# Closing the MLP's small tiles early and reordering the first four token tiles in a fused attention and MLP kernel

## Chip, cores and metric

The kernel runs on one core of a Trainium2 chip. The metric is the device time of one execution in microseconds (us). The engines are named as the profile names them: PE is TensorE (PEld its weight loads), DVE is VectorE, ACT is ScalarE, POOL is GpSimd, SP is SyncE, which here only issues transfers.

## What is computed

A layer norm of x feeds two branches, whose outputs are added to x: a recurrent attention over 64 segments of 32 tokens that carries 8 memory rows from segment to segment, and a dense MLP with GELU.

```python
x = A_x                      # 1 x 2048 x 1024, bf16
xn = _layernorm(x, axis=-1)
return x + _A_ref(xn, A_mem0, A_Wq, A_Wk, A_Wv, A_Wo, 32) + _B_ref(xn, B_w1, B_b1, B_w2, B_b2)

# _A_ref, for each of the 64 segments:
h = concat([mem, xs])                     # 8 + 32 rows
q, k, v = h @ Wq, h @ Wk, h @ Wv          # 32 heads of 128
p = softmax(where(mask, q @ k.T * scale, -1e9))
o = (p @ v) @ Wo
mem = o[:, :8]                            # goes to the next segment
# _B_ref: gelu(xn @ w1 + b1) @ w2 + b2, with 3584 hidden columns
```

## The kernel before

**Two stages.** The MLP is done first (lines 299 to 614), then a loop over the 64 segments (line 691 on). The four attention matrices are cut into 64 units of 512 KB each. 46 of them stay in SBUF for the whole loop (resident). 18 are streamed: two are copied from PSUM by DVE, and 16 are transferred again from DRAM in each segment, one of these only in part. Streamed units live in six slots (`RING`); when PE has used one, `start_stream` (line 246) issues the transfer of the unit that is due six places later into the same slot.

**The first token tiles.** The MLP goes over four groups of four token tiles (128 tokens each). For a tile, `ln_stats` (line 348) makes two `bn_stats` of 512 columns and an aggregate on DVE, `ln_sqrt` a square root on ACT and `ln_rstd` a reciprocal on DVE. The normalised tile `ln_xn` is then made by `ln_apply_scalar` on ACT (line 371) for tiles 0 to 2 of the first group, and by `ln_apply` on DVE (line 363) for tile 3. `turn_x` (line 383) turns it with eight PE transposes into PSUM and copies it out in two halves, one on ACT and one on DVE. `begin`, `normed` and the loop at line 472 order these so that the statistics of tile t+1 come ahead of the application of tile t. Only after all four tiles does PE begin the first product (line 509): for each of 28 blocks of hidden columns (`fb`), eight matmuls of 512 columns. ACT, DVE and ACT again then make the GELU.

**SP's queue** holds its transfers in program order and waits at the first one that may not go yet. Apart from these waits the program lets each hardware transfer wait for the one issued eight before it. At the start the order is: four tiles of x, two pairs of w1, the bias `b1rows`, the other pairs of w1, then w2.

**Where the units go.** SBUF is full during the MLP. When the last group (`tg == 3`) has used a piece of w1, w2 or the GELU result `gT`, its place is given to a resident unit: `fetch_resident("w1_..")` at line 535 and, within the last second products (line 595: 28 steps `fc`, eight matmuls each), `w2_..` at line 606 and `gT..` at line 608. Four units (`LATE`, tiles `W_O..`, parts of Wo) have no such place. They go into the pool `late` (line 621), which takes the address range that the MLP's small tiles (pool `ma`: `g_xb`, `g_u`, `ln_xn`, `ones`, `b2row` and others) had, and so is opened after `ma` is closed. Their transfers, then those of two units in `xt2` and `xt3`, are put in `late_units` (line 672), and `unit_done` (line 675) issues one of them after each streamed unit that the first segment uses:

```python
            if IS_STREAMED[unit]:
                start_stream(slot_of.pop(place_in_stream.pop(unit)))
                if late_units:
                    late_units.popleft()()
```

`xt2` and `xt3` hold the last four token tiles until `keep_R` has stored them (`R_n`, issued by ACT at line 415), so their transfers wait for these stores.

**The first segment** (s = 0) makes nearly every product twice (for the rows of the segment, `hr_home`, and for rows left over from the neighbours, `hrL`). The order of the passes is K, Q, K, Q, V, V and then the output product O.

**The end.** In the last segment the result leaves in 12 small transfers, dealt out in turn to SP, ACT and POOL (line 1049).

Of the kernel before, what the change touches and what calls it, by code (L numbers as in the profile page):

```python
# [51 lines left out]
LATER = 3  # L52
LAG = 3
STREAM_BUFS = 6
AT_BANKS, AT_PART = 5, 4
PART_COLS = 768

# [30 lines left out]
def kernel(  # L88
# [208 lines left out]


    NT = S // P
    with tc.tile_pool(name="ma", bufs=2) as ma, tc.tile_pool(name="mps", bufs=6, space=PSUM) as mps:  # L300
        eps_t = ma.tile([P, 1], F32, name="eps_t", bufs=1)
        nc.vector.memset(eps_t[:], EPS)
        ones = ma.tile([1, P], BF16, name="ones", bufs=1)
# [21 lines left out]
                w1_sb.append(t)  # L325

        b1rows = ma.tile([FC, P], BF16, name="b1rows", bufs=1)
        load_w1(range(2))
        nc.sync.dma_start(out=b1rows[:, :], in_=B_b1.rearrange("(fc p) -> fc p", p=P))
        load_w1(range(2, 6))  # L330
        masks_out()
        for j in range(4):
            nc.sync.dma_start(
# [11 lines left out]
        mv = ma.tile([P, NT, 2], F32, name="ln_mv", bufs=1)  # L345
        rstd = ma.tile([P, NT], F32, name="ln_rstd", bufs=1)

        def ln_stats(tt, xt):
            stats = ma.tile([P, 2, 6], F32, name="ln_stats")
            for c in range(2):  # L350
                nc.vector.bn_stats(out=stats[:, c, :], in_=xt[:, c * 512:c * 512 + 512])
            nc.vector.bn_aggr(out=mv[:, tt, :], in_=stats[:, :, :])

        def ln_sqrt(t0, t1):
            nc.scalar.activation(
                out=rstd[:, t0:t1], in_=mv[:, t0:t1, 1:2].rearrange("p t o -> p (t o)"), func=ACT.Sqrt,
                bias=eps_t[:, :], scale=1.0,
            )
# [9 lines left out]
            )  # L368
            return xn

        def ln_apply_scalar(tt):

            xn = ma.tile([P, DM], BF16, name="ln_xn")
            shift = mv[:, tt, 0:1]
            nc.vector.tensor_scalar(
                out=shift, in0=shift, scalar1=rstd[:, tt:tt + 1], scalar2=-1.0, op0=ALU.mult, op1=ALU.mult,
            )
            nc.scalar.activation(
                out=xn[:, :], in_=xtoks[tt], func=ACT.Identity, bias=shift, scale=rstd[:, tt:tt + 1],
            )  # L380
            return xn

        def turn_x(tt, xn, xnT):
            t = tt % 4
            pT = mps.tile([P, KT, P], BF16, name="pT", bufs=2)
            for kt in range(KT):
                nc.tensor.transpose(pT[:, kt, :], xn[:, kt * P:(kt + 1) * P], ident)
            for half in range(2):
                cp = nc.scalar.copy if (tt + half) % 2 else nc.vector.tensor_copy
                cp(  # L390
                    out=xnT[half][:, 4 * t:4 * t + 4, :, :].rearrange("p s k t -> p k s t"),
                    in_=pT[:, 4 * half:4 * half + 4, :].rearrange("p k (s t) -> p k s t", t=SEG),
                )

        def keep_xT(tg, xnT):
            xl = [sp.tile([P, 2, KT, GRP, NL], BF16, name="xl", tag=("a", "kL0")[k]) for k in range(2)]
# [62 lines left out]
            ]  # L459

        xnT = new_xnT(0)
        def begin(tt):
            ln_stats(tt, xtoks[tt])
            ln_sqrt(tt, tt + 1)

        def normed(tt):
            ln_rstd(tt, tt + 1)
            return ln_apply_scalar(tt) if tt < 3 else ln_apply(tt)

        begin(0)  # L470
        xns = []
        for tt in range(4):
            if tt < 3:
                begin(tt + 1)
            xns.append(normed(tt))
            if tt > 0:
                turn_x(tt - 1, xns[tt - 1], xnT)
        turn_x(3, xns[3], xnT)
        keep_xT(0, xnT)

        b1col = ma.tile([P, FC], F32, name="b1col", bufs=1)
# [6 lines left out]
        for tg in range(4):  # L488
# [16 lines left out]

            pend = None
            for fb in range(FC):
                ps = mps.tile([P, 512], F32, name="ps")
                for kt in range(KT):
                    nc.tensor.matmul(  # L510
                        ps[:, :].rearrange("p (s t) -> p s t", t=SEG),
                        lhsT=w1_sb[fb // 2][:, kt, (fb % 2) * P:(fb % 2 + 1) * P],
                        rhs=xnT[kt // 4][:, :, kt % 4, :],
                        start=(kt == 0),
                        stop=(kt == KT - 1),
                    )
                xb = ma.tile([P, 512], BF16, name="g_xb", bufs=3)
                nc.scalar.activation(  # L518
                    out=xb[:, :], in_=ps[:, :], func=ACT.Identity, bias=b1col[:, fb:fb + 1], scale=1.0
                )  # L520
                u = ma.tile([P, 512], BF16, name="g_u")
                nc.vector.tensor_tensor(out=u[:, :], in0=xb[:, :], in1=xb[:, :], op=ALU.mult)
                nc.vector.tensor_scalar(
                    out=u[:, :], in0=u[:, :], scalar1=0.044715, scalar2=1.0, op0=ALU.mult, op1=ALU.add
                )
                nc.vector.tensor_tensor(out=u[:, :], in0=u[:, :], in1=xb[:, :], op=ALU.mult)  # L526
                if pend is not None:
                    gelu_tail(*pend)
                pend = (fb, u, xb)
                if last and fb % 2:  # L530
                    place = f"w1_{fb // 2}"
                    if place in RING:
                        start_stream(place)
                    else:
                        fetch_resident(place)
# [9 lines left out]
            if not last:  # L545
# [5 lines left out]
                        fetch(c, unit)  # L551
                    fetch_resident(*EARLY)
                for t in range(4):
                    ln_stats(4 * tg + 4 + t, xtoks[4 * tg + 4 + t])
                ln_sqrt(4 * tg + 4, 4 * tg + 8)
                ln_rstd(4 * tg + 4, 4 * tg + 8)
                for t in range(4):
# [22 lines left out]
            else:  # L580
# [8 lines left out]
                for n in range(8):  # L589
                    cs = slice((n % 2) * 512, (n % 2 + 1) * 512)  # L590
                    nc.tensor.matmul(pss[n][:, :], lhsT=ones[0:1, :], rhs=b2row[0:1, cs], start=True, stop=False)
                    nc.tensor.matmul(
                        pss[n][:, :], lhsT=ident, rhs=xtoks[4 * tg + n // 2][:, cs], start=False, stop=False
                    )
                for fc in range(FC):
                    for t in range(4):
                        for nb in range(2):
                            nc.tensor.matmul(
                                pss[2 * t + nb][:, :],
                                lhsT=gts[fc // 4][:, fc % 4, t * P:(t + 1) * P],  # L600
                                rhs=w2_sb[fc // 2][:, fc % 2, nb * 512:nb * 512 + 512],
                                start=False,
                                stop=(fc == FC - 1),
                            )
                    if fc % 2:
                        fetch_resident(f"w2_{fc // 2}")
                    if fc % 4 == 3:
                        fetch_resident(f"gT{fc // 4}")
# [9 lines left out]

    with tc.tile_pool(name="late", bufs=1) as late, \
            tc.tile_pool(name="banks", bufs=1, space=PSUM) as banks:
        nc.scalar.preload_act_table_set("natural_log_exp_and_others")

        small = deque()
# [38 lines left out]
                return stream_tiles.pop(used - 1)[:, :]  # L664
            return res_tiles[unit]

        def fetch_late(unit):
            t = late.tile([P, 2048], BF16, name="W_" + "_".join(map(str, unit)))[:, :]
            res_tiles[unit] = t
            fetch(t, unit)  # L670

        late_units = deque(lambda unit=unit: fetch_late(unit) for unit in LATE)
        late_units += [lambda: fetch_resident("xt2"), lambda: fetch_resident("xt3")]

        def unit_done(unit):

# [14 lines left out]
        for s in range(NSEG):  # L691
# [354 lines left out]
            ]  # L1046
            left_rows = [(sl, row) for sl, row in left_rows if row >= 0]
            if final:
                engines = [nc.sync, nc.scalar, nc.gpsimd]
                n = 0  # L1050
                for w, r in enumerate(tiles):
                    for b in range(2):
                        cs = slice(256 * (2 * b + w), 256 * (2 * b + w) + 256)
                        pieces = [(rows, slice(64 * b + m0, 64 * b + m0 + NX))]
                        for sl, row in left_rows:
                            p0 = 64 * b + NL * sl
                            pieces.append((slice(row, row + NL), slice(p0, p0 + NL)))
                        for o, i in pieces:
                            engines[n % 3].dma_start(out=out_flat[o, cs], in_=r[i, :])
                            n += 1  # L1060
            elif left_o:
                pairs = [(out_flat[rows, :], outL_d[og, m0:m0 + NX, :])]
                pairs += [
                    (out_flat[row:row + NL, :], outL_d[og, NL * sl:NL * sl + NL, :]) for sl, row in left_rows
                ]
                for o, r in pairs:
                    small.append(lambda o=o, r=r: nc.gpsimd.dma_start(out=o, in_=r))
            else:
                for j in range(4):
                    nc.gpsimd.dma_start(out=out_flat[rows, 256 * j:256 * j + 256], in_=res[32 * j:32 * j + NX, :])  # L1070
# [37 lines left out]
```

## Time and profile before

| | us |
|---|---|
| three runs | 1865.07, 1869.99, 1869.29 (median 1869.29) |
| profiled execution | 1868.06 |
| its span, first to last instruction | 1866.3 |
| begin of the first product of the MLP | 15.99 |
| end of the last second products | 418.2 |
| first product of the segment loop | 419.35 |
| last matmul | 1859.84 |
| PE busy, share of the span | 92% |
| DVE, ACT, POOL busy | 48%, 35%, 15% |
| bytes moved by transfers | 613 MB |

The profile gives busy times of the engines, and a chain of waits that is followed back from the last instruction. A matmul's row has a start and a modelled end, and the ends of neighbours overlap: the distance of starts is the rate at which they go. In a timeline, "x8" is a merged row of eight instructions, and the bracket names the idle time before it and what ended it. DMA share is the mean busy share of 16 transfer engines; it can be a little over 1. Times are counted from the start of the span.

### The profile page before, as it was taken

The page shows a single profiled execution, that of the slowest core. Times are in us where ns is not written, and L with a number is a line of the kernel's source. Part 1 is how long each engine was busy: PE and PEld are TensorE (multiplying, and loading weights), DVE is VectorE, ACT ScalarE, POOL GpSimd, SP SyncE. Part 2 cuts the span into 40 slices and gives each one's busy share as a digit, 9 for nine tenths or more (in the row PEclk, how much of TensorE's full clock was granted, in tenths as well). Part 3 has the DMA queues.
Part 4 walks back from the last instruction along what each step waited for, and adds up shares of the span by engine and source line. Part 5 has one row for each costly group of instructions (what it writes and reads, how often), then busy time and mean ns, then how long its engine had stood idle before and what let it go on. Part 6 is the DMA issues. An engine that isn't in the chain of part 4 may idle for free.

```text
span 1866.3 us, 72877 instructions
## 1 busy us (share of the span) xinstructions
PE 1720.2 (92%) x32208; PEld 938.3 (50%) x32228; DVE 905.1 (48%) x2192; ACT 649.4 (35%) x1382; POOL 286.7 (15%) x563
## 2 busy tenths in 40 slices
PE   7999999999999999998899999999898898999987
PEld 3444444445555555555554555555555454545544
DVE  6657483705444444444444444444444444445443
ACT  6434251602333333333333333333333333333333
POOL 0000001401341121111111111111111111111112
PEclk9999999999999999999999999999999999999999
DMA  9921212769999999999999999999999999999998
GB/s 290 311 83 47 54 46 60 255 217 388 401 394 380 395 390 384 387 380 371 369 383 368 390 388 390 365 384 374 379 389 360 369 368 377 387 389 394 388 381 315
DMA packets 229353, 613.13 MB, mean 329 GB/s; under 512 B 46859, under 2 KB 76091, under 8 KB 229036
## 3 DMA queue, kind: packets, MB, share of 16 engines
q1 hardware_dynamic: 207260, 588.06, 83.8%
q0 software_dynamic: 17536, 17.71, 2.9%
q8 instruction: 252, 4.13, 0.9%
q10 hardware_dynamic: 4240, 2.71, 0.5%
q14 instruction: 65, 0.53, 0.1%
HBM read 594.40 MB, written 29.23 MB: 334 GB/s over the span
## 4 chain that ended last, share of the span: by engine, by line
PE 40%; DMA 20%; issue 4%; DVE 4%; ACT 2%; POOL 0%; DVEq 0%; ACTq 0%; SPq 0%; POOLq 0%
PE acc L715 27%; PE acc L919 9%; DMA u<-Wc_K 8%; DMA u<-Wc_O 7%; DMA outL_d<-half_home 2%; PE acc L891 1%; DMA u<-Wc_Q 1%; ACT mixed L865 1%; DVE b_oL L780 1%; PE mixed L824 1%; DVE pd_main L872 1%; DMA u<-Wc_V 1%; DMA hr_home<-hr_d 1%; ACT mixed L862 0%; PE mixed L830 0%
## 5 line engine op out<-in xcount | busy, mean ns | idle before, releaser
L715 PE MATMUL acc<-u,hr_home 128*32 128x512 bf16 x11520 | 781.3, 381 | 36.6 <-issue 13.8
L715 PEld LDWEIGHTS <-hr_home 128*32 128x32 bf16 x12288 | 353.3, 96 | 321.8 <-issue 69.7
L715 PE MATMUL acc<-u,hrL 128*32 128x512 bf16 x2880 | 258.7, 383 | 7.7 <-issue 7.3
L510 PE MATMUL ps<-u 128*128 128x512 bf16 x896 | 195.5, 381 | 2.6 <-ACT u L390 2.6
L244 DVE TENSOR_SCALAR u<-kept 128x512 uint32<-128x512 uint32 x254 | 163.4, 685 | 33.1 <-PE acc L715 11.1
L919 PE MATMUL acc<-u,d_oL 128*32 128x256 bf16 (+1 forms) x3108 | 157.6, 290 | 22.5 <-DMA u<-Wc_O 12.8
L565 PE MATMUL ps<-u 128*128 128x512 bf16 x657 | 146.2, 379 | 0.8
L919 PEld LDWEIGHTS <-b_oL 128*32 128x32 bf16 x3569 | 112.8, 98 | 67.4 <-issue 36.7
L1070 POOL DMA_DIRECT2D out_dram<-hr_home x188 | 96.3, 513 | 310.3 <-DVE hr_home L1037 296.9
L510 PEld LDWEIGHTS <-u 128*128 128x128 bf16 x896 | 88.1, 98 | 108.8 <-issue 4.8
L919 PEld LDWEIGHTS <-d_oL 128*32 128x32 bf16 (+1 forms) x3552 | 104.4, 98 | 74.9 <-issue 34.9
L872 DVE TENSOR_TENSOR pd_main<-half_home,mixed 128x320 bf16<-128x320 bf16 x128 | 62.5, 488 | 153.5 <-ACT mixed L865 152.2
L919 PE MATMUL acc<-u,b_oL 128*32 128x256 bf16 (+2 forms) x2062 | 119.9, 289 | 18.4 <-DMA u<-Wc_O 10.6
L266 POOL DMA_DIRECT2D hr_home<-hr_d x58 | 32.8, 565 | 589.3 <-PE acc L715 570.0
L780 DVE STREAM_TRANSPOSE b_oL<-b_oL 128x512 bf16<-128x512 bf16 x128 | 90.6, 708 | 63.0 <-ACT b_oL L766 63.0
L715 PEld LDWEIGHTS <-hrL 128*32 128x32 bf16 x3072 | 91.8, 96 | 58.3 <-issue 22.3
L766 ACT CAST kT<-acc 128x512 bf16<-128x512 f32 x64 | 37.5, 586 | 217.2 <-PE acc L715 217.2
L766 ACT CAST b_oL<-acc 128x512 bf16<-128x512 f32 x128 | 75.2, 587 | 83.6 <-PE acc L715 82.6
L565 PEld LDWEIGHTS <-u 128*128 128x128 bf16 x672 | 65.3, 98 | 77.4 <-DVE g_u L526 0.4
L1022 ACT CAST d_oL<-acc 128x256 bf16<-128x256 f32 (+1 forms) x63 | 26.9, 427 | 211.8 <-PE acc L919 211.8
L518 ACT ACTIVATE g_xb<-ps,b1col 128x512 bf16<-128x512 f32 x112 | 76.8, 686 | 60.4 <-PE ps L510 59.3
L865 ACT ACTIVATE mixed<-mixed,small_consts 128x160 f32<-128x160 f32 x256 | 94.2, 368 | 8.4
(127 smaller groups left out, 2004.7 us busy)
## 6 DMA issues: line engine op xcount, KB each, us to landing
u<-Wc_K SPq DMA_DIRECT2D x320, 512.0 KB
u<-Wc_V SPq DMA_DIRECT2D x256, 512.0 KB
u<-Wc_O SPq DMA_DIRECT2D x256, 512.0 KB
u<-Wc_Q SPq DMA_DIRECT2D x128, 512.0 KB
u<-Wc_O SPq DMA_DIRECT2D x64, 320.0 KB
u<-in_B_w_dram SPq DMA_DIRECT2D x28, 512.0 KB
hr_home<-hr_d POOLq DMA_DIRECT2D x58, 128.0 KB, 5.5
u<-in_A_Wq_dram SPq DMA_DIRECT2D x14, 512.0 KB
```

The source lines that it names most:

```text
L244: nc.vector.tensor_single_scalar(out=out, in_=in_, scalar=0, op=ALU.bitwise_or)
L266: eng.dma_start(out=hr_home[:, 0:n], in_=hr_d[s, :, 0:n])
L510: nc.tensor.matmul(ps[:, :].rearrange("p (s t) -> p s t", t=SEG), lhsT=w1_sb[fb // 2][:, kt, (fb % 2) * P:(fb % 2 + 1) * P], rhs=xnT[kt // ...
L518: nc.scalar.activation(out=xb[:, :], in_=ps[:, :], func=ACT.Identity, bias=b1col[:, fb:fb + 1], scale=1.0)
L565: nc.tensor.matmul(ps[:, :], lhsT=gts[fc // 4][:, fc % 4, t * P:(t + 1) * P], rhs=w2_sb[fc // 2][:, fc % 2, cs], start=(fc == 0), stop=(fc ...
L715: nc.tensor.matmul(o, lhsT=lhs[:, i, :], rhs=m, start=(i == seq[0]), stop=(i == seq[-1]), tile_position=(0, 32 * j),)
L766: cp(out=out, in_=ps.rearrange("p (h e) -> p h e", e=32))
L780: nc.vector.transpose(out=home, in_=home)
L865: nc.scalar.activation(out=mixed[:, 160 * b:160 * b + 160], in_=mixed[:, 0:160], func=ACT.Exp, scale=-1.0, bias=off[:, b:b + 1],)
L872: nc.vector.tensor_tensor(out=pdA.rearrange("p c b q -> p b c q"), in0=prA[:, None, :, :].to_broadcast([P, 2, 4, 40]), in1=dd, op=ALU.mult,)
L919: nc.tensor.matmul(acc[r:r + n // 8, c:c + wide], lhsT=lhs[:, 4 * (i % 4) + 2 * u + k, :], rhs=w_t[:, c0 + c:c0 + c + wide], start=(unit = ...
L1070: nc.gpsimd.dma_start(out=out_flat[rows, 256 * j:256 * j + 256], in_=res[32 * j:32 * j + NX, :])
```

## The change

Three things are changed.

1. The pool `ma` is entered in an exit stack of its own, `mlp`, which is closed in the last group after the matmuls that put bias and residual into the eight PSUM tiles and before the 28 steps of the last second products. `late` is opened there, and the four `LATE` units are issued on SP at once. `late_units` keeps only `xt2` and `xt3`.
2. The first four token tiles: 16 matmuls on the identity are issued on PE first, with a result that nobody reads (`idle`). Statistics are made in halves (`ln_half`) between the other steps; all four tiles are applied by DVE; both halves of a turned tile are copied out by ACT, except one of tile 3. The first product of the column blocks 0 and 1 is made for tiles 0 and 1 (segments 0 to 7, matmuls of 256 columns) between the transposes of tile 2 and tile 3, that of block 2 after the transposes of tile 3. The loop over `fb` then makes only the other half of these three. The bias `b1rows` goes ahead of the second pair of w1 in SP's queue.
3. The 12 transfers at the end go to SP and ACT alone.

```diff
+WARM = 16
...
+    mlp = ctx.enter_context(ExitStack())
+    with tc.tile_pool(name="mps", bufs=6, space=PSUM) as mps:
+        ma = mlp.enter_context(tc.tile_pool(name="ma", bufs=2))
...
-        load_w1(range(2))
+        load_w1(range(1))
         nc.sync.dma_start(out=b1rows[:, :], in_=B_b1.rearrange("(fc p) -> fc p", p=P))
-        load_w1(range(2, 6))
+        load_w1(range(1, 6))
...
+        def first_product(ps, fb, xnT, s0, s1):
+            for kt in range(KT):
+                nc.tensor.matmul(
+                    ps[:, SEG * s0:SEG * s1].rearrange("p (s t) -> p s t", t=SEG),
+                    lhsT=w1_sb[fb // 2][:, kt, (fb % 2) * P:(fb % 2 + 1) * P],
+                    rhs=xnT[kt // 4][:, s0:s1, kt % 4, :],
+                    start=(kt == 0),
+                    stop=(kt == KT - 1),
+                )
...
+        idle = new_ps()
+        for _ in range(WARM):
+            nc.tensor.matmul(
+                idle.rearrange("p (a b) -> p a b", b=P), lhsT=ident, rhs=ident[:, None, :].to_broadcast([P, 4, P]),
+                start=True, stop=True,
+            )
+        begun = [new_ps() for _ in range(3)]
+        ln_stats(0)
+        ln_half(1, 0)
+        ln_sqrt(0, 1)
+        pTs = []
+        for tt in range(4):
+            ln_rstd(tt, tt + 1)
+            pTs.append(turned(ln_apply(tt)))
+            if tt < 3:
+                ln_half(tt + 1, 1)
+                turned_out(tt, pTs[tt], 0, xnT, nc.scalar.copy)
+                ln_sqrt(tt + 1, tt + 2)
+                turned_out(tt, pTs[tt], 1, xnT, nc.scalar.copy)
+            if tt < 2:
+                ln_half(tt + 2, 0)
+            if tt == 2:
+                for fb in range(2):
+                    first_product(begun[fb], fb, xnT, 0, 8)
+        turned_out(3, pTs[3], 0, xnT, nc.vector.tensor_copy)
+        turned_out(3, pTs[3], 1, xnT, nc.scalar.copy)
+        first_product(begun[2], 2, xnT, 0, 8)
...
+                if tg == 0 and fb < len(begun):
+                    ps = begun[fb]
+                    first_product(ps, fb, xnT, 8, 16)
+                else:
+                    ps = new_ps()
+                    first_product(ps, fb, xnT, 0, 16)
...
+                mlp.close()
+                late = ctx.enter_context(tc.tile_pool(name="late", bufs=1))
+                for unit in LATE:
+                    res_tiles[unit] = late.tile([P, 2048], BF16, name="W_" + "_".join(map(str, unit)))[:, :]
+                    fetch(res_tiles[unit], unit)
                 for fc in range(FC):
...
-        late_units = deque(lambda unit=unit: fetch_late(unit) for unit in LATE)
-        late_units += [lambda: fetch_resident("xt2"), lambda: fetch_resident("xt3")]
+        late_units = deque([lambda: fetch_resident("xt2"), lambda: fetch_resident("xt3")])
...
-                engines = [nc.sync, nc.scalar, nc.gpsimd]
+                engines = [nc.sync, nc.scalar]
...
-                            engines[n % 3].dma_start(out=out_flat[o, cs], in_=r[i, :])
+                            engines[n % 2].dma_start(out=out_flat[o, cs], in_=r[i, :])
```

More of the change, by code (lines that the diff above doesn't have):

```diff
@@ L299 @@
     NT = S // P
-    with tc.tile_pool(name="ma", bufs=2) as ma, tc.tile_pool(name="mps", bufs=6, space=PSUM) as mps:
+    mlp = ctx.enter_context(ExitStack())
+    with tc.tile_pool(name="mps", bufs=6, space=PSUM) as mps:
+        ma = mlp.enter_context(tc.tile_pool(name="ma", bufs=2))
         eps_t = ma.tile([P, 1], F32, name="eps_t", bufs=1)
@@ L346, with ln_half, ln_stats @@
         rstd = ma.tile([P, NT], F32, name="ln_rstd", bufs=1)
[L348 to L352, printed above, removed]
+        half_stats = {}
+        def ln_half(tt, c):
+            if c == 0:
+                half_stats[tt] = ma.tile([P, 2, 6], F32, name="ln_stats")
+            nc.vector.bn_stats(out=half_stats[tt][:, c, :], in_=xtoks[tt][:, c * 512:c * 512 + 512])
+            if c == 1:
+                nc.vector.bn_aggr(out=mv[:, tt, :], in_=half_stats.pop(tt)[:, :, :])
+        def ln_stats(tt):
+            ln_half(tt, 0)
+            ln_half(tt, 1)
         def ln_sqrt(t0, t1):
@@ L369, in ln_apply, with turned @@
             return xn
[L371 to L384, printed above, removed]
+        def turned(xn):
             pT = mps.tile([P, KT, P], BF16, name="pT", bufs=2)
@@ L387, in turn_x, with turned_out @@
                 nc.tensor.transpose(pT[:, kt, :], xn[:, kt * P:(kt + 1) * P], ident)
-            for half in range(2):
[L389 to L393, printed above, removed]
+            return pT
+        def turned_out(tt, pT, half, xnT, cp):
+            t = tt % 4
+            cp(
+                out=xnT[half][:, 4 * t:4 * t + 4, :, :].rearrange("p s k t -> p k s t"),
+                in_=pT[:, 4 * half:4 * half + 4, :].rearrange("p k (s t) -> p k s t", t=SEG),
+            )
+        def turn_x(tt, xn, xnT):
+            pT = turned(xn)
+            for half in range(2):
+                turned_out(tt, pT, half, xnT, nc.scalar.copy if (tt + half) % 2 else nc.vector.tensor_copy)
         def keep_xT(tg, xnT):
@@ L461, with new_ps @@
         xnT = new_xnT(0)
[L462 to L466, printed above, removed]
+        def first_product(ps, fb, xnT, s0, s1):
[7 more added lines that the diff above has]
+                )
+        def new_ps():
+            return mps.tile([P, 512], F32, name="ps")
+        idle = new_ps()
[3 more added lines that the diff above has]
+                start=True, stop=True,
+            )
+        begun = [new_ps() for _ in range(3)]
[4 more added lines that the diff above has]
+        for tt in range(4):
             ln_rstd(tt, tt + 1)
[L468 to L472, printed above, removed]
+            pTs.append(turned(ln_apply(tt)))
             if tt < 3:
[L474 to L478, printed above, removed]
+                ln_half(tt + 1, 1)
[10 more added lines that the diff above has]
+        first_product(begun[2], 2, xnT, 0, 8)
         keep_xT(0, xnT)
@@ L507 @@
             for fb in range(FC):
[L508 to L516, printed above, removed]
+                if tg == 0 and fb < len(begun):
[4 more added lines that the diff above has]
+                    first_product(ps, fb, xnT, 0, 16)
                 xb = ma.tile([P, 512], BF16, name="g_xb", bufs=3)
@@ L553 @@
                 for t in range(4):
-                    ln_stats(4 * tg + 4 + t, xtoks[4 * tg + 4 + t])
+                    ln_stats(4 * tg + 4 + t)
                 ln_sqrt(4 * tg + 4, 4 * tg + 8)
@@ L614 @@
                     keep_R(4 * tg + t, xtoks[4 * tg + t])
-    with tc.tile_pool(name="late", bufs=1) as late, \
-            tc.tile_pool(name="banks", bufs=1, space=PSUM) as banks:
+    with tc.tile_pool(name="banks", bufs=1, space=PSUM) as banks:
         nc.scalar.preload_act_table_set("natural_log_exp_and_others")
@@ L665, in unit_tile @@
             return res_tiles[unit]
[L667 to L670, printed above, removed]
-        late_units = deque(lambda unit=unit: fetch_late(unit) for unit in LATE)
-        late_units += [lambda: fetch_resident("xt2"), lambda: fetch_resident("xt3")]
+        late_units = deque([lambda: fetch_resident("xt2"), lambda: fetch_resident("xt3")])
         def unit_done(unit):
```

## The prediction, made before the changed kernel was run

> **What bounds the kernel now.** I read the slices of the page first, then windows of equal length, then the timelines of the three places that the change touches.
>
> The slices:
>
> ```profile
> PE   7999999999999999998899999999898898999987
> DMA  9921212769999999999999999999999999999998
> ```
>
> PE is busy nearly everywhere. The transfers are idle for most of the MLP (slices 3 to 8) and full through the whole segment loop. So the MLP is bound by PE; the loop needs both, and while transfers are full, a byte moved out of the loop into the MLP is worth its transfer time. Windows around the border (columns: stretch, its length, busy us of PE, PEld, DVE, ACT and POOL with counts, granted PE clock, DMA share, GB/s):
>
> ```profile
> 400.00:410.00 10.00, 10.00 (x48) 4.56 (x47) 0.00 (x0) 0.00 (x0) 0.00 (x0) 1.00 0.76 248
> 410.00:420.00 10.00, 8.84 (x51) 3.92 (x53) 3.14 (x5) 2.05 (x4) 0.00 (x0) 1.00 0.60 190
> 430.00:440.00 10.00, 8.27 (x183) 4.39 (x173) 5.60 (x12) 2.48 (x6) 0.00 (x0) 1.00 1.04 398
> 440.00:450.00 10.00, 8.62 (x192) 4.75 (x195) 2.29 (x7) 2.75 (x7) 0.59 (x1) 0.83 1.04 401
> ```
>
> In the last second products (to 418.2) a quarter to 40% of the transfer time is free; in the first segment none is, PE loses time, and its clock falls for a while. At about 400 GB/s a unit of 512 KB takes 1.31 us. PE's timeline there:
>
> ```profile
> 437.83 0.83 PE L715 MATMUL acc<-u,hr_home 128*32 128x512 bf16 x12
> 440.64 0.40 PE L715 MATMUL acc<-u,hr_home 128*32 128x512 bf16 x4 [1.97 <-DMA u<-Wc_V]
> 442.51 0.65 PE L715 MATMUL acc<-u,hrL 128*32 128x512 bf16 x4
> 443.27 0.62 PE L715 MATMUL acc<-u,hr_home 128*32 128x512 bf16 x4
> ```
>
> and SP's queue (start, us, what it issues):
>
> ```profile
> 366.10 0.38 SPq L586 DMA_DIRECT2D d_oL<-in_A_Wo_dram  x1
> 373.38 10.69 SPq L225 DMA_DIRECT2D u<-in_A_Wq_dram  x5
> 423.40 0.38 SPq L223 DMA_DIRECT2D W_O<-in_A_Wo_dram  x1
> 431.17 0.38 SPq L223 DMA_DIRECT2D u<-in_A_Wo_dram  x1
> ```
>
> A streamed part of Wv comes 1.97 us late while four late W_O units and two xt units stand between the streams. After that PE runs at half clock (0.61 in 442 to 443.5, 0.50 in 443.5 to 445.5). SP issues nothing from 366.5 to 373.4.
>
> The start, PE alone:
>
> ```profile
> 8.12 1.04 PE L387 MATMUL pT<-hr_home,ln_xn 128*128 128x128 bf16 x8 [8.12 <-ACT ln_xn L378]
> 12.70 1.04 PE L387 MATMUL pT<-hr_home,ln_xn 128*128 128x128 bf16 x8 [1.84 <-ACT ln_xn L378]
> 15.99 4.26 PE L510 MATMUL ps<-u 128*128 128x512 bf16 x12 [0.54 <-ACT u L390]
> ```
>
> PE has nothing but transposes until 15.99, since it waits for tiles that ACT makes. Then its first seven matmuls start 0.427 us apart and from 19.0 on 0.216 us apart. From there to 418 it has hardly a gap, so an earlier start moves the whole MLP.
>
> [...]
>
> **Part 1, late units.** Four transfers of 512 KB leave the first segment: 4 x 1.31 = 5.2 us of a full resource. They go where SP idled. In program order they stand behind d_oL (366.1) and wait for DVE and PE instructions that touch the old small tiles; the last readers are the GELU's last DVE product (ends 367.7) and the bias matmuls of L591 (ends 369.6). So they issue from about 369.7 to 371.2 (0.38 us each), ahead of the w2 places that PE frees from 373.4. The 50 us that follow move 21 units, 11 MB; 2.1 MB more lift the share from about 0.7 to about 0.8. The w2 and gT places go on being freed by PE every 3.5 us, and nothing fetched there is used before 419. Cost in the MLP: nothing, covered by the idle transfers; if that cover were gone, 1.31 us for each unit.
>
> What is late next in the first segment? Streams no longer alternate with W_O, but xt2 and xt3 move up to the first and third place of SP's order behind the Q streams, and they wait for the R_n stores that ACT issues at 418.4 to 420.9. Behind them in SP's queue stand Q and all V streams. About 2.8 MB (two residents, four stores, a part of Wo and a Q stream) are ahead or beside; at 300 to 400 GB/s from 418.3 plus about 2 us of landing, the last store is in by 427 to 430. The V streams, issued at 426.5, 429.3, 430.2 and 432.4 before, then go from 429 on, but with two instead of five foreign units among them: I place them at 435.0, 436.3, 437.6 and 438.9. PE wants the third at 438.5 and the fourth at about 440.5. So the waits go.
>
> On PE's path this gives the wait at 435.37 (0.30), 1.97, the gap before 443.27 (0.3) and the slow clock: 3.4 us at half rate less the gap, about 1.3 us. Sum 3.9 us by 446. Then at the start of segment 1 PE waited 0.7 us for Wc_K, and 1.5 us for Wc_O until 500. Here the transfers are the limit, and they have gained up to 5.2 us. So the loop gains between 3.9 and 5.2 us; I take 4.8. It keeps it to the end because from there on both resources are merely shifted. If the R_n wait held SP until 432, V would still be late by about 1.5 us and the gain about 3.
>
> **Part 2, the start.** x is there at 3.59 as before. Step by step: statistics of tile 0 (1.29 and 0.21) end at 5.1, the half of tile 1 (0.62) at 5.7, with the square root (0.29) beside; reciprocal 0.11, application on DVE 0.55 instead of 1.24 on ACT: tile 0 is ready at 6.5 instead of 8.06. The 16 idle matmuls start at 1.45, when the identity is there. Seven cold ones (3.0 us) and nine warm (1.9) would end at 6.4, all cold (6.8) at 8.3. I take 6.9, so 0.4 us of delay. From one tile's transposes to the next: transposes 0.61 warm to 1.04 cold, first ACT copy 0.56, square root 0.29, reciprocal 0.11, application 0.55, some 0.3 of handing over: 2.4 to 2.8 us. Tile 2's transposes start at 11.9 and end at 12.6. Then 16 matmuls of 256 columns: 1.7 warm, 3.4 cold. Here the clock decides. Between 7 and 12 PE has only transposes, and before, transposes alone did not raise the clock. I take it as cold for most of this piece: 15.3. Tile 3 was ready at about 14; its transposes end at 16.1, the third half product at 17.0, the copies (0.59) beside it. Then three halves (3 x 0.87) and 25 whole blocks (25 x 1.728): 17.0 + 2.6 + 43.2 = 62.8, against 65.94 before (L542). Gain 3.2 us; wholly warm it is 5.1, wholly cold 1.9. I take 3.4. The cover for the rest: the second w1 pair goes behind b1rows, whose row on SP took 2.67 us, but is wanted only at 16; later pairs are issued at about 1.5 us each (L324, eight in 11.85) while PE uses one in 3.46; x of the next tiles is issued at 57.2 to 58.7, landing by some 63, and DVE would ask for it at 65.7.
>
> **Part 3, the end.**
>
> ```profile
> 1861.89 0.72 SPq L1059 DMA_DIRECT2D out_dram<-half_home  x2
> 1862.07 1.00 POOL L1059 DMA_DIRECT2D out_dram<-half_home  x2
> ```
>
> Six issues of 0.35 to 0.45 us on SP and ACT from 1860.66 end at about 1863.2; POOL's last ended at 1863.07. The ninth to twelfth wait for a landing eight earlier, but by then it has come. I take 0.3 us of loss, bounds -0.5 and +0.6.
>
> **Sum.** -3.4 - 4.8 + 0.3 = -7.9 us. Against the profiled execution (span 1866.3, 1.8 us around it, 1868.06) that is 1860.2; against the median 1869.29 it is 1861.4. I name 1860.5.
>
> **Rivals.** A, the forecast: both gains come, 1860.5, chance 0.69. B: the loop gains, the start does not (cold clock, the idle matmuls in the way): 1868.1 - 4.8 + 0.3 = 1863.6, chance 0.13; for it speaks that transposes left PE cold before. C: the start gains, but the loop takes back its 5 us, since PE is at 0.91 of each 90 us of the loop and may set the pace where transfers dip (340 GB/s at 690 to 697): 1868.1 - 3.4 + 0.3 = 1865.0, chance 0.09; against it speak the full transfers from 425 to 565. D: slower. SP holds still at the first W_O because a small tile is let go of late. Up to about 408 this costs nothing; if it held until the second products end at 417.6, 25 units would crowd into the first segment, whose transfers then need some 43 x 1.3 = 56 us instead of about 33 (22 units and the stores): 1868.1 - 3.4 + 20 = 1885, chance 0.05. Against it: the instructions that it waits for stand before the 28 steps in program order. E: the best end of every bound, 5.1, 5.2 and 0.5 us: 1857.3, chance 0.04.
>
> **How the numbers follow.** Two runs of this kernel differ by up to 0.3% (5.6 us), so 1863.7 is the border of faster. A lies below it nine times in ten, B in under half, E always, C seldom: faster 0.72, same 0.22, slower 0.06. Range 1855.5 to 1865.5: from E less a run's scatter of about 2 us up to B and C.
>
> **What would show it.** L469, the 256 wide products, begins at about 12 and its distance of starts is 0.213 or 0.108; the first 512 wide one at about 19.5; L542's successor at about 62.5. W_O issues at about 366 on SP in the new time, no wait over 0.5 us for Wc_V in the first segment, no half clock there, and this segment shorter by 4 us. I am wrong if SP waits long at xt3, if the loop's length from segment 2 on grows, or if W_O appears behind w2.

## The result, and the profile after

The changed kernel takes 1866.41 us (median of 22 executions, 1856.37 to 1876.95) beside 1872.63 us of the kernel before in the same measurement (22 executions, 1862.63 to 1884.88). The ratio is 0.9959 with a 95% interval of 0.9938 to 0.998. Measured a second time it is 0.9964 (0.9947 to 0.9981). The two together, weighted by their intervals, give 0.9962 ± 0.0013, which is 7.1 us of 1871 (4.6 to 9.6). The forecast was 7.9 us faster. The kernel before came out 3.3 us higher here than in the three executions on which the forecast stood, so the ratio is the fair comparison. Taken absolutely, the median lies 0.9 us above the top of the forecast range (1855.5 to 1865.5). The profiled execution took 1860.83 us, its span 1859.1; that it falls so near to the 1860.5 that was named is chance, with single executions from 1856 to 1877.

The slices of the page after:

```profile
PE   8999999999989999989998999899998989989987
DMA  9931212779999999999999999999999999999997
```

Slice 9 of the transfers, with the last second products, has risen from 6 to 7: the late units now lie there. SP's queue after shows where (start, us, what it issues):

```profile
363.27 0.38 SPq L611 DMA_DIRECT2D d_oL<-in_A_Wo_dram  x1
366.48 1.92 SPq L224 DMA_DIRECT2D W_O<-in_A_Wo_dram  x4
370.25 10.69 SPq L226 DMA_DIRECT2D u<-in_A_Wq_dram  x5
...
418.10 0.42 SPq L258 DMA_DIRECT2D u<-Wc_Q  x1
424.05 0.38 SPq L224 DMA_DIRECT2D u<-in_A_Wo_dram  x1
424.48 0.46 SPq L258 DMA_DIRECT2D u<-Wc_Q  x1
426.66 0.38 SPq L224 DMA_DIRECT2D u<-in_A_Wo_dram  x1
427.45 1.75 SPq L258 DMA_DIRECT2D u<-Wc_V  x4
```

The four W_O units go out at 366.5, at once after the MLP's small tiles are let go, and the next issue stands where it stood (370.25; 373.38 before, with the whole MLP 3.1 us later). In the first segment SP stands still from 418.5 to 424.05 at the first of the two xt units, which waits for the `R_n` stores, with a Q stream and all V streams behind it. PE's timeline in that segment shows what this costs:

```profile
430.03 0.40 PE L738 MATMUL acc<-u,hr_home 128*32 128x512 bf16 x4 [0.53 <-DMA u<-Wc_Q]
433.00 0.40 PE L738 MATMUL acc<-u,hr_home 128*32 128x512 bf16 x4 [0.51 <-DMA u<-Wc_V]
```

Two waits of half a microsecond stand where one of 0.30 and one of 1.97 stood. A window of the last second products before (columns as in the prediction)

```profile
370.00:380.00 10.00, 9.95 (x47) 4.52 (x47) 0.00 (x0) 0.00 (x0) 2.22 (x4) 1.00 0.58 181
```

and after, with two of the first segment:

```profile
370.00:380.00 10.00, 9.95 (x48) 4.52 (x47) 0.00 (x0) 0.00 (x0) 0.00 (x0) 1.00 0.98 357
430.00:440.00 10.00, 9.46 (x212) 5.13 (x215) 5.18 (x12) 3.09 (x8) 0.00 (x0) 1.00 0.99 383
440.00:450.00 10.00, 8.15 (x209) 5.22 (x205) 4.82 (x10) 2.14 (x6) 2.66 (x5) 1.00 0.98 354
```

From 370 to 380 the late units fill what was free (0.98 of the transfer time instead of 0.58), and PE goes on without a gap. From 430 to 440 PE makes 212 matmuls instead of 183 (the stage lies 3 us further on in this trace), and its clock stays whole. The transfers still read 0.99 and 0.98 of their time as busy, though they move only 383 and 354 GB/s there. The start, PE alone:

```profile
1.43 5.64 PE L482 MATMUL ps<-hr_home 128*128 128x512 bf16 x16 [1.43 <-POOL hr_home masks.py:199]
6.91 0.61 PE L384 MATMUL pT<-hr_home,ln_xn 128*128 128x128 bf16 x8
9.17 0.62 PE L384 MATMUL pT<-hr_home,ln_xn 128*128 128x128 bf16 x8 [1.65 <-DVE ln_xn L375]
11.53 0.62 PE L384 MATMUL pT<-hr_home,ln_xn 128*128 128x128 bf16 x8 [1.73 <-DVE ln_xn L375]
11.98 3.24 PE L469 MATMUL ps<-u 128*128 128x256 bf16 x16
15.01 0.99 PE L384 MATMUL pT<-hr_home,ln_xn 128*128 128x128 bf16 x8
15.83 1.04 PE L469 MATMUL ps<-u 128*128 128x256 bf16 x8
16.92 6.25 PE L469 MATMUL ps<-u 128*128 128x256 bf16 x40
```

The transposes run warm (0.61 us for eight), then the granted clock is 0.50 (12.4 to 15.8) and the 16 half products take 3.24 us; the eight after tile 3 run warm again (1.04 us), and the second halves begin at 16.92. The end:

```profile
1853.95 1.03 SPq L1082 DMA_DIRECT2D out_dram<-hr_home  x3
1853.95 1.28 ACTq L1082 DMA_DIRECT2D out_dram<-hr_home  x3
1855.15 0.98 SPq L1082 DMA_DIRECT2D out_dram<-half_home  x3
1855.33 0.98 ACTq L1082 DMA_DIRECT2D out_dram<-half_home  x3
```

### The profile page after: what moved, and what is told of

Its sections match the earlier page's. It is cut to its first block, busy times and chain, and to the rows that moved or that the text cites. A ratio compares the mean times of both kernels' runs of the same rounds, so it can differ in the third digit from the quotient of the medians.

```text
span 1859.1 us, 72948 instructions
## 1 busy us (share of the span) xinstructions
PE 1724.0 (93%) x32248; PEld 941.6 (51%) x32268; DVE 905.3 (49%) x2189; ACT 646.7 (35%) x1382; POOL 284.5 (15%) x559
## 4 chain that ended last, share of the span: by engine, by line
PE 71%; DMA 18%; issue 4%; DVE 4%; ACT 3%; POOL 0%; DVEq 0%; ACTq 0%; SPq 0%; POOLq 0%
PE acc L738 34%; PE acc L942 11%; PE ps L469 10%; DMA u<-Wc_K 10%; PE ps L590 8%; DMA u<-Wc_O 4%; PE ps L628 2%; PE acc L914 2%; DMA u<-Wc_V 2%; DMA outL_d<-half_home 1%; ACT mixed L888 1%; PE mixed L847 1%; DVE b_oL L803 1%; DVE pd_main L895 1%; PE pT L628 1%
## 5 line engine op out<-in xcount | busy, mean ns | idle before, releaser
L469 PE MATMUL ps<-u 128*128 128x512 bf16 (+1 forms) x920 | 195.8, 375 | 2.0 <-ACT u L389 2.0
L590 PE MATMUL ps<-u 128*128 128x512 bf16 x657 | 146.2, 379 | 0.8
L942 PE MATMUL acc<-u,b_oL 128*32 128x256 bf16 (+2 forms) x2062 | 120.9, 291 | 14.3 <-DMA u<-Wc_O 6.8
L267 POOL DMA_DIRECT2D hr_home<-hr_d x58 | 32.8, 565 | 588.8 <-PE acc L738 582.7
L803 DVE STREAM_TRANSPOSE b_oL<-b_oL 128x512 bf16<-128x512 bf16 x128 | 90.6, 708 | 62.8 <-ACT b_oL L789 62.8
```

The source lines that it names most:

```text
L469: nc.tensor.matmul(ps[:, SEG * s0:SEG * s1].rearrange("p (s t) -> p s t", t=SEG), lhsT=w1_sb[fb // 2][:, kt, (fb % 2) * P:(fb % 2 + 1) * P ...
L590: nc.tensor.matmul(ps[:, :], lhsT=gts[fc // 4][:, fc % 4, t * P:(t + 1) * P], rhs=w2_sb[fc // 2][:, fc % 2, cs], start=(fc == 0), stop=(fc ...
L803: nc.vector.transpose(out=home, in_=home)
L942: nc.tensor.matmul(acc[r:r + n // 8, c:c + wide], lhsT=lhs[:, 4 * (i % 4) + 2 * u + k, :], rhs=w_t[:, c0 + c:c0 + c + wide], start=(unit = ...
```

## The experiments

Theory: part 2 shifts a MLP that hangs on PE and this lasts; part 1 wins in the first segment and keeps what it wins, since the transfers bound the loop. Rival: segments 1 to 5 take back the gain of the loop or of the start.

### The parts alone

`late_only` is the kernel before with part 1 alone, `start_only` with part 2 alone; each keeps the rest of the kernel before, its end too. Their edits are those pieces of the change. Both were measured twice, the second time as `late_again` and `start_again`.

> Part 1 alone: the pool closed early and the four W_O units fetched in the last second products; start and end as in the kernel before. If transfers bound the whole segment loop, the gain of about 3 to 5 us at the first segment's end is kept to the last matmul: 3.9 to 5.2 us faster than before. If PE or the six stream slots set the pace from segment 2 or 3 on, the gain is there at the end of segment 0 (about 3 us) and is down to about 1 us by segment 5 and at the end: 0 to 1.5 us faster.

> Part 2 alone: idle matmuls, statistics in halves, all four tiles on DVE, half products begun early; late units and the end as in the kernel before. The MLP hangs on PE alone, so both theories expect the first product of the loop 3.1 us earlier than before. If transfers are the limit of the loop, the whole loop is only moved and the time is 3 us shorter; if the transfers that the MLP leaves to the loop's first segments set their pace, the 3 us are given back there and the time is within 1 us of before.

> The changed kernel again, on one chip with its parts. If the parts add up, its gain is that of the late units plus that of the start, plus 0.4 us at the tail: with a lasting loop gain 7 to 8.5 us, with a loop gain that is absorbed 3.5 to 5 us.

> Part 1 alone, measured again for its size: the first time it was 2 to 3 us faster, between the 4.8 us that I predicted and the 0 to 1.5 us of a gain that is absorbed. With both together: 4 to 5 us if a byte less in the first segment is worth its transfer time to the end, 2 to 3 us if about half of it stays.

> Part 2 alone, measured again: the first 14 executions gave 1 us faster with an error of 2. If the earlier MLP lasts, 3 us and with the first ones over 2; if the loop takes it back, within 1 us of before. The profile also shows whether the half products meet the half clock (second halves at 16.9) or not (15.5).

| | first ratio (95%) | second ratio (95%) | together, of 1871 us |
|---|---|---|---|
| part 1 alone | 0.9988 (0.9971 to 1.0004) | 0.9979 (0.9962 to 0.9997) | 3.0 us faster (0.8 to 5.3) |
| part 2 alone | 0.9989 (0.9967 to 1.0011) | 0.9983 (0.9965 to 1.0002) | 2.7 us faster (0.1 to 5.4) |
| all three | 0.9959 (0.9938 to 0.998) | 0.9964 (0.9947 to 0.9981) | 7.1 us faster (4.6 to 9.6) |

The parts add up within their errors: 3.0 + 2.7 and the end's 0.7 (below) are 6.4 of 7.1. Part 1 is smaller than the 4.8 us forecast, though that value is inside its interval; part 2 is about what was forecast.

### More references, and where the time goes by segment

Single profiles of one kernel differ by up to 22.6 us in the span (start_only 1876.9, start_again 1854.3), so the kernel before was profiled twice more.

> The kernel before, profiled again, as a second reference for the loop. If the first trace of it was a usual one, the first product of the loop comes at 419.4 (or up to 3.5 us later with a half clock stretch at about 366), and segments 1 to 5 after it take 107 us as there. If that trace was a lucky one, they take 109 to 112 us as in most traces of the changed kernel, and then nothing was given back there.

> The same once more, a third reference: segments 1 to 5 take 107 us again if the changed kernel gives part of its gain back in them, 109 to 112 us if the first trace was a lucky one.

The table takes from each trace the first product of the loop, the end of segment 0 (when ACT has copied its memory rows out), and the length of segments 1 to 5 together, up to the point in segment 5 where ACT begins to wait for its memory rows (5.0 to 5.2 us before they are out, in every trace); the last column is PE's half clock in the MLP after the warm-up.

| execution | first product | segment 0 | segments 1 to 5 | half clock, us |
|---|---|---|---|---|
| before | 419.35 | 33.2 | 107.0 | none |
| before_1 | 423.21 | 32.8 | 107.0 | 6.83 from 368.7 |
| before_2 | 423.26 | 32.6 | 107.5 | 6.83 from 368.7 |
| late_only | 423.58 | 29.6 | 106.7 | 6.83 from 369.3 |
| late_again | 419.58 | 29.9 | 107.1 | none |
| start_only | 415.91 | 32.7 | 110.2 | 3.41 from 11.7 |
| start_again | 416.78 | 33.0 | 110.3 | 3.41 from 364.9 |
| after | 416.23 | 30.1 | 111.2 | 3.41 from 12.4 |
| after_again | 416.11 | 31.1 | 111.0 | 3.41 from 12.1 |
| extra_mid | 416.64 | 30.1 | 112.4 | 3.41 from 364.6 |
| more_each | 416.47 | 31.0 | 111.7 | 3.41 from 364.4 |
| less_each | 418.11 | 30.0 | 107.4 | 6.83 from 364.3 |
| no_warm | 416.91 | 29.5 | 108.7 | none |
| fill_xt | 415.70 | 29.4 | 112.2 | 3.41 from 363.7 |

Three things are read from it. Part 1 shortens segment 0 by about 3 us: 32.6 to 33.2 without it, 29.4 to 31.1 with it, and the two groups do not overlap. Part 2 as it is (seven executions) brings the loop's first product 2.9 us forward on average against the two executions of the old start without a half clock. And in seven of nine executions with part 2, segments 1 to 5 take 3 to 5 us longer than the 106.7 to 107.5 of all five without it. In three of the seven (extra_mid, more_each, fill_xt) PE also went at half clock there, for 3.4 to 6.8 us; in the other four it did not. So the first trace of before was not a lucky one there. These two windows, each of segments 1 to 5, show the same work at another rate. The first is before_1:

```profile
456.00:563.00 107.00, 98.03 (x2267) 55.48 (x2257) 50.05 (x121) 37.08 (x86) 43.70 (x80) 1.00 1.02 396
```

and the second is the changed kernel:

```profile
446.40:557.60 111.20, 99.81 (x2267) 55.25 (x2261) 50.09 (x122) 36.99 (x86) 44.79 (x82) 1.00 1.00 382
```

PE has 2267 matmuls in both, and the bytes are the same (107.0 us x 396 GB/s and 111.2 us x 382 GB/s are 42.4 and 42.5 MB), so the transfers went at a lower rate while their share still reads full. Why they do stays open; no run here tells it. The program alone does not fix it: less_each is the changed kernel unaltered up to segment 8, and it shows next to no loss. Its first product is also the latest of the nine (418.11), so the new start and an early arrival at the loop are not told apart. For the whole of part 2, its mean lead at the first product, 5.2 us (five old starts 421.8, the seven with part 2 as it is 416.6), less the mean loss of 3.5 (110.6 against 107.1), leaves 1.7 us, which lies inside the interval of the 2.7 measured.

### What a byte is worth in the loop

`extra_mid` adds 12 transfers of 512 KB in one place, `more_each` one of 256 KB in each of 48 segments, `less_each` takes 256 KB away in each of 48 segments; all three are edits of the changed kernel. In `less_each` half of one unit of Wv isn't fetched, and the product reads the other half twice.

```diff
 extra_mid, in unit_done; more_left is 12 from s == 20
+                if more_left[0]:
+                    more_left[0] -= 1
+                    nc.sync.dma_start(out=spare_d[more_left[0]][:, :], in_=copies["K", 0, 0])
```

> The changed kernel with 12 more transfers of 512 KB from DRAM to DRAM, one behind each of 12 successive streamed units from segment 20 on, with a result that nobody reads: the price of a byte in the loop. If transfers are the limit there, each costs its 1.25 to 1.3 us and the time grows by about 15 us, all in segments 20 and 21, and it stays to the end. If the loop is held by PE with a little slack in the transfers, part is made up within a few segments and the time grows by 4 to 10 us.

```diff
 more_each, in unit_done; one entry for each segment from 8 to 55
+                if more_left:
+                    nc.sync.dma_start(out=spare_d[more_left.pop() % 12][:, 0:1024], in_=copies["K", 0, 0][:, 0:1024])
```

> The changed kernel with one more transfer of 256 KB (half a unit, DRAM to DRAM, a result that nobody reads) in each of 48 segments, 8 to 55: 12.6 MB. If the transfers alone bound the loop, each costs half of 1.2 to 1.3 us, together 29 to 31 us. If PE and transfers set the pace in turn and a segment has slack of its own, clearly less: 10 to 20 us.

```diff
 less_each; half_of is the unit ("V", 4, 0)
-            nc.sync.dma_start(out=t[:, :], in_=copies[unit])
+            if unit == half_of and 8 <= streams[:n].count(unit) < 56:
+                nc.sync.dma_start(out=t[:, 0:1024], in_=copies[unit][:, 0:1024])
+            else:
+                nc.sync.dma_start(out=t[:, :], in_=copies[unit])
...
+                    jj = j % 2 if t is half_tile[0] else j
-                    o, m = acc[32 * j:32 * j + 32, :], t[:, 512 * j:512 * j + 512]
+                    o, m = acc[32 * j:32 * j + 32, :], t[:, 512 * jj:512 * jj + 512]
```

> The changed kernel with the transfer of one streamed unit of Wv cut to its first half in 48 segments, 8 to 55; the product then reads the first half twice, so that V is another one, and PE's work is the same. 12.6 MB less. If the transfers alone bound the loop, it is 29 to 31 us faster than the changed kernel. If PE and transfers set the pace in turn, a byte taken away is worth less than its transfer time: 10 to 20 us. If PE is the bound, 0 to 5.

Each has a ratio to the kernel before, from which the changed kernel's is subtracted (0.9964 of the same measurement for extra_mid, 0.9962 for the others).

| | ratio to before (95%) | against the changed kernel, us | for each 512 KB |
|---|---|---|---|
| 12 x 512 KB more, one place | 1.0015 (0.9996 to 1.0034) | +9.5 (4.8 to 14.3) | 0.8 |
| 48 x 256 KB more, spread | 1.0024 (1.0007 to 1.0041) | +11.6 (7.6 to 15.6) | 0.48 |
| 48 x 256 KB less, spread | 0.9931 (0.9907 to 0.9955) | -5.8 (-10.9 to -0.7) | 0.24 |

None comes near 1.31 us a unit except inside the one crowded segment: in the trace of `extra_mid`, segment 20 takes 35.2 us instead of 21.6, which is 1.13 us for each of the 12, with 11.5 us of half clock in it. Spread out, a byte added costs about a third of its transfer time and a byte taken away brings about a fifth. These two are not the same kind of transfer: nothing waits for the added ones, which go from DRAM to DRAM, while a product waits for the stream that was cut; and their intervals overlap. Both lie far below the 31 us (an estimate: 24 units at 1.31) that transfers as the only bound would give. So the transfers alone do not bound the loop. A window of 150 us in the loop shows why the share misled. Before:

```profile
1500.00:1650.00 150.00, 137.36 (x3162) 77.82 (x3154) 69.67 (x167) 49.34 (x113) 22.08 (x42) 1.00 0.99 376
```

With less_each:

```profile
1500.00:1650.00 150.00, 136.08 (x3133) 76.35 (x3129) 70.02 (x167) 50.18 (x116) 24.25 (x47) 1.00 0.99 368
```

The share is 0.99 in both, though one moves fewer bytes; and in more_each from 1350 to 1500 it is 1.02 at 397 GB/s. So a share near 1 does not tell that no more could be moved. The rate tells more: 376 GB/s, where single windows of 10 us in the kernel before reached 398 and 401.

### The start

`no_warm` is the changed kernel with `WARM = 0`. `fill_xt` is meant to hold PE's clock between the tiles and also moves the two xt units back:

```diff
-WARM = 16
+WARM = 13
+FILL = 6
...
             pTs.append(turned(ln_apply(tt)))
+            if tt < 2:
+                keep_warm(FILL)
...
-        late_units = deque([lambda: fetch_resident("xt2"), lambda: fetch_resident("xt3")])
+        late_units = deque([lambda: None] * 4 + [lambda: fetch_resident("xt2"), lambda: fetch_resident("xt3")])
```

Here `keep_warm(n)` issues n of the idle matmuls.

> The changed kernel without its 16 idle matmuls. My prediction's step has them in the way for 0.4 us and PE cold for the half products in any case: then tile 0's transposes begin at 6.45 instead of 6.91, run at half clock like all that follow until 15.8, and the second halves begin within 0.4 us of 16.9. If the idle matmuls are worth something, transposes of 1.04 instead of 0.61 us in three tiles move the second halves to 17.3 to 18.

> The changed kernel with 13 idle matmuls ahead and 6 more after the transposes of tile 0 and of tile 1, which hold the clock, and with xt2 and xt3 fetched four streamed units later. Head: the 16 half products take 1.75 instead of 3.24 us and the second halves begin at about 15.3 instead of 16.9, so the loop's first product comes 1.6 us earlier, about 414.6; if the clock falls in spite of it, nothing there. First segment: no stop of SP from 418 to 424, so the waits for Wc_Q and Wc_V of 0.5 us each go and its end comes up to 1 us earlier in addition. Whole kernel: 1.5 to 2.6 us faster than the changed kernel if it lasts; 0 to 1 if the loop takes back what is won before segment 5.

PE's timeline of no_warm:

```profile
6.38 1.03 PE L384 MATMUL pT<-hr_home,ln_xn 128*128 128x128 bf16 x8 [6.38 <-DVE ln_xn L375]
...
12.66 3.57 PE L469 MATMUL ps<-u 128*128 128x256 bf16 x16
...
17.59 6.68 PE L469 MATMUL ps<-u 128*128 128x256 bf16 x42
```

Tile 0 goes 0.53 us earlier, as the first theory had it, but the transposes of three tiles take 1.03 to 1.04 us instead of 0.61 and the half products 3.57 instead of 3.24, and the second halves begin at 17.59 instead of 16.92. In these two traces the idle matmuls are worth 0.7 us even where the clock falls after them. In start_again the same start did not meet the fall:

```profile
12.46 1.91 PE L467 MATMUL ps<-u 128*128 128x256 bf16 x16
...
15.89 6.46 PE L467 MATMUL ps<-u 128*128 128x256 bf16 x41
```

The half products take 1.91 instead of 3.24 us and the second halves begin at 15.89. Of the seven starts with the 16 idle matmuls, three met the fall at about 12 and four did not. fill_xt:

```profile
11.38 1.91 PE L470 MATMUL ps<-u 128*128 128x256 bf16 x16
...
14.80 9.48 PE L470 MATMUL ps<-u 128*128 128x256 bf16 x55
```

The second halves begin 2.1 us earlier than in the changed kernel's trace, more than the 1.6 expected. But the loop's first product came at 415.70, only 0.5 earlier, since this execution met a half clock of 3.41 us at 363.7. SP's queue of fill_xt in the first segment:

```profile
417.57 2.22 SPq L259 DMA_DIRECT2D u<-Wc_Q  x2
419.91 4.86 SPq L259 DMA_DIRECT2D u<-Wc_V  x3
424.87 0.38 SPq L225 DMA_DIRECT2D u<-in_A_Wo_dram  x1
```

SP no longer stops: the Q and V streams are out before xt2, PE waits for neither, and segment 0 takes 29.4 us, the shortest of all. The whole kernel has the ratio 0.9954 (0.9935 to 0.9974). Against 0.9962 of the changed kernel that is 1.5 us faster with an interval from 5.9 faster to 3 slower: not told apart.

## Why the prediction was right, point by point

The sum was 7.9 us, measured 7.1 (4.6 to 9.6), and the likeliest case, A, is the one that came. That the sum is so close is in part luck: part 1 came out 1.8 us smaller than forecast and part 2 0.7, while part 3, forecast as a loss of 0.3, gained 0.7. Rival D is out: SP was not held, W_O went at 366.48 where "about 366" was named. B is out in the traces: the start gained. C, in which the loop takes its gain back, came in part, but not as it was named: what is given back in segments 1 to 5 goes with the new start and not with the late units. Two of the signs of being wrong showed: SP stood 5.5 us at the first xt unit, and segments 2 to 5 took 2.3 us longer than before in the pair of traces. The scatter of a run, taken as about 2 us, was too small, and so were the 0.3% (5.6 us) between two runs: 22 executions of the changed kernel lie 20.6 us apart.

**Part 2, 3.4 us.** The step "the second halves at 17.0" measured 16.92; the MLP's first stage ends at 62.81 (forecast 62.8); the loop's first product is 3.12 us earlier in the pair of traces; the time is 2.7 us less. "Here the clock decides" was right, and "I take it as cold" was right for three executions in seven. The 1.7 us warm and 3.4 cold for the 16 half products were an estimate, 16 times half of 0.216 and of 0.427 us; they took 1.91 and 3.24. Where it stayed warm, one us was won at the start, and the half clock came at 364 instead: start_again's first product, 416.78, is no earlier than that of the traces with the fall at 12. The 0.4 us that the idle matmuls delay tile 0 were there (0.53); what they bring the step did not say, and against no_warm they bring 0.7.

**Part 1, 4.8 us.** The mis-sized term. Segment 0 is shorter by 3 us and the time by 3.0 (0.8 to 5.3). Two pieces of the term failed. First, the 1.3 us for the slow clock after the wait at 440 (granted clock 0.50 for 3.41 us, 442.33 to 445.74): before_1 and before_2 have the waits for Wc_V too and no half clock there, and their segment 0 is only 0.4 to 0.6 us shorter. PE's waits in before_1 from 423 to 456 (us in total, times, longest):

```profile
PE acc L715 <- DMA u<-Wc_V: 2.4, 2, 2.0
PE acc L919 <- DMA u<-Wc_O: 0.8, 2, 0.4
```

The wait for Wc_O (0.6 us in before_2) is not among the waits of the first trace: what PE wins there without the half clock it seems to lose, in part, at the next transfer. Without this piece the path sum is 0.30 + 1.97 + 0.3 = 2.6 us, near what came. Second, the value of the bytes: "while transfers are full, a byte moved out of the loop into the MLP is worth its transfer time", and so up to 5.2 us beyond the first segment. Four units at 3.0 us are 0.75 each, and the byte runs give 0.24 to 0.8. The step "it keeps it to the end" holds for what was left: segments 1 to 5 of late_only and late_again are as long as before, 106.7 and 107.1. The hold of SP at the R_n stores was foreseen, but it lasted longer (V was to be issued from 429 on in the old time, about 425.9 in the new, and went from 427.45 on), and its cost was put at nothing: it was half a microsecond for Wc_V and another for Wc_Q (0.9 and 0.8 in after_again), which the step did not name.

**Part 3, 0.3 us of loss.** The sign failed. From the last matmul to the end of the span, seven traces with three issuers take 6.25 to 6.79 us (mean 6.51), seven with two 5.47 to 6.02 (mean 5.84): 0.7 us won. The step had the issues end later; they do not: the last one ends 3.18 us after the last matmul in the changed kernel's trace, and POOL's last one ended 3.23 us after it before. What follows is shorter too. The packets in the traces show a part of it: the last packet of these transfers ends 3.95 to 3.96 us after the last matmul in the seven traces with POOL, whose packet it is, and 3.76 to 3.77 in the seven without. That is 0.2 of the 0.7 us; the rest lies behind the last packet, and what it is stays open.

## What to carry to other kernels

A transfer share of 1.00 is no proof that transfers bound a loop (here it read 0.99 at 376 and at 368 GB/s, and 1.02 at 397): compare the GB/s with the highest that the same kernel reaches, and price a byte by adding and taking away some before moving it. The wait that was removed from the first segment was worth about the wait itself here, not the transfer time of what was moved. Where two profiles of one kernel differ more than the gain sought, sort executions by stages that repeat (here the first product of the loop and segment 0) and judge the whole by many timed executions.

## What the runs showed of the hardware

The half clock also comes while PE is busy. Near 365 no long gap precedes it, as PE's timeline of less_each shows:

```profile
363.46 0.37 PE L620 MATMUL ps<-b2row,ones 1*128 1x512 bf16 x1
363.76 0.39 PE L621 MATMUL ps<-u,hr_home 128*128 128x512 bf16 x1
364.08 0.42 PE L620 MATMUL pT<-b2row,ones 1*128 1x512 bf16 x1
364.44 0.61 PE L621 MATMUL pT<-u,hr_home 128*128 128x512 bf16 x1
```

These are the matmuls that put bias and residual into PSUM; in every second one the input has a single row (1*128). The longest gap ahead of it is 0.26 us, yet from 364.3 on PE goes at half clock for 6.83 us (granted 0.50 from 365 to 370, 1.00 from 355 to 360) and loses half of that. It came in 8 of 14 traces, always towards the end of this piece; in the others it did not come, though the piece is the same. What sets it off was not shown: no run here changes this piece.

By half of the 3.41 or 6.83 us at half clock, the spell is estimated to cost 1.7 to 3.4 us of an execution, as much as either part of the change.
